# One load queue, ten transposes on TensorE, spread norms and a searched TensorE order, in a mixer-plus-MLP kernel

## The chip, the cores and the metric

The kernel runs on one core of one Trainium2 chip. The metric is the device time of one execution in microseconds. The profile shows the span from the first to the last instruction, 2.1 us (before) less than that time. Every run carries a state, fast or slow, set against the fastest run of the same kernel in the same group of runs. The engines are TensorE (PE), VectorE (DVE), ScalarE (ACT), GpSimd (POOL) and SyncE (SP); SyncE only issues DMAs here.

## The reference, cut to what matters

```python
B, S, D, F = 1, 2048, 512, 1792           # bf16 throughout
h  = gelu(layernorm(x) @ w1)              # [2048, 512]
hs = shifted(h) @ w2                      # each quarter of h moved by 1, -1, 2, -2 tokens
x1 = x + hs
out = x1 + gelu(layernorm(x1) @ w3) @ w4  # w3 [512, 1792], w4 [1792, 512]
```

The 2048 tokens are 16 tiles of 128. In units of one 128x128 by 128x512 matmul the four products need 64 + 64 + 224 + 224 = 576.

## The kernel before

Each tile is normalized (statistics on VectorE, the reciprocal root on ScalarE for tiles 0 to 3 and on GpSimd for the rest), transposed so that the features lie on partitions, multiplied ("up"), passed through GELU on ScalarE, and multiplied again ("mix" in layer 1, "down" in layer 2). A small list scheduler fixes the order of every engine. PE's order is given by a script; the other engines are ordered by a priority and a rough model of durations. Engines run their lists strictly in order.

```python
PE_TP = (0, 1, 2, 3, 4, 5)      # these tiles are transposed by PE, all others by DMA
NORM_ACT = (6, 7)               # these norms run on ScalarE, all others on VectorE
SCRIPT = """
warm:9 tp:0 warm:3 tp:1 up1:0 up1:1 tp:2-3 up1:2 mix:0-1 tp:4-5 up1:3 mix:2-3 up1:4 up2:0 mix:4-5 up2:1 mix:6
up1:5 down:0 mix:7 down:1-3 up2:2 mix:8 up1:6 ...      # cut
"""
...
loads = [load_x("sp", 0, 1), load_x("sp", 1, 1), load_w("sp", "w1", w1_sb, w1, 0, 2),
         load_w("sp", "w1", w1_sb, w1, 2, 4), load_x("sp", 2, 1), load_x("sp", 3, 1),
         load_x("sp", 4, 2), load_x("sp", 6, 2), load_w("sp", "w2", w2_sb, w2, 0, DC)]
...
load_w("pool", "w3", w3_sb, w3, 0, DC, after=[(("x", 1), 0)])
load_x("pool", 8, 4, after=[(("x", 7), 0)])
load_x("pool", 12, 4, after=[(("w3", 0), 0)])
load_w("pool", "w4", w4_sb, w4, 0, 7, after=[(("xT", 2, 1), 0)])
load_w("pool", "w4", w4_sb, w4, 7, 14, after=[(("xT", 2, 1), 0)])
```

`up1:g` and `up2:g` are the up-projections of a group of tiles in layers 1 and 2. `up2:0` covers tiles 0 and 1, `up2:1` tiles 2 and 3. "warm" are useless matmuls that keep PE busy until data come. DMA transposes are issued by SyncE, in the same queue as its loads.

## Time and profile before

| | before |
|---|---|
| time, median of the first 4 runs | 153.74 us (150.10 to 157.47) |
| span of the profiled run, its mean clock | 151.6 us, 0.966 |
| PE busy | 137.7 us, 91% |
| 576 matmuls at 216 ns | 124.3 us |
| start of the second w3 group (`up2:1`) | 39.06 us |

First the busy line and the slices of the page of the kernel before. The slices cut the span into 40 equal parts of 3.79 us; a digit is the busy share in tenths, and PEclk is the granted clock.

```profile
PE 137.7 (91%) x730; PEld 71.0 (47%) x730; DVE 62.1 (41%) x162; ACT 45.9 (30%) x54; POOL 20.8 (14%) x43
PE   6925959996699999999999999999969999999993
DVE  2816679898913253110045866691001100012321
PEclk9997589999879999999999999999999999999999
```

PE is full from the twelfth slice to the end but for the thirtieth slice, a wait for GELU, and the last. Most of the loss lies in the first eleven slices, and in two places the clock is below 9.

Next, lines of the timeline of PE before: start, duration, engine, line, operation, output<-inputs, count, and in brackets the idle time before it and what ended it.

```profile
6.66 1.95 PE L314 MATMUL y_ps<-xnT,w_sb 128*128 128x128 bf16 x32
12.41 1.13 PE L290 MATMUL o_ps<-ident,xn_buf 128*128 128x128 bf16 x8 [3.80 <-DVE xn_buf L275]
14.23 3.60 PE L314 MATMUL y_ps<-xnT,w_sb 128*128 128x256 bf16 x16 [0.69 <-ACT xnT L295]
22.83 1.92 PE L314 MATMUL y_ps<-xnT,w_sb 128*128 128x256 bf16 x16 [1.05 <-ACT xnT L295]
39.06 1.14 PE L314 MATMUL y_ps<-x1nT,w_sb 128*128 128x256 bf16 x9 [2.57 <-DMA x1nT<-xn_buf]
112.67 6.20 PE L378 MATMUL o_ps<-w_sb,h2T 128*128 128x512 bf16 x28 [1.21 <-ACT h2T L329]
```

The 3.80 us gap waits for the norm of tile 2. The same 16 matmuls take 3.60 us at 14.23 and 1.92 us at 22.83: the first time the clock is at half. The 2.57 us gap before `up2:1` waits for a DMA transpose. (The line at 39.06 is cut off by the end of the view's window at 40 us: the whole group is 56 matmuls and takes 7.94 us in the chain of waits.)

Why the norm of tile 2 came so late is read from VectorE's timeline of the kernel before:

```profile
5.90 0.69 DVE L247 BATCH_NORM_STATS2 st<-x_sb 128x6 f32<-128x512 bf16 x1
6.86 0.69 DVE L247 BATCH_NORM_STATS2 st<-x_sb 128x6 f32<-128x512 bf16 x1
11.15 0.69 DVE L247 BATCH_NORM_STATS2 st<-x_sb 128x6 f32<-128x512 bf16 x1 [3.38 <-DMA x_sb<-in_x_dram]
11.95 0.41 DVE L275 TENSOR_SCALAR xn_buf<-x_sb,mv,rstd 128x512 bf16<-128x512 bf16 x1
```

The statistics of tiles 2 and 3 were done by 7.6 us, and ScalarE had their roots by 8.1 us.

Two lines of the chain that ended last, before (start, duration, what), name the causes of the two gaps:

```profile
3.64 7.49 DMA x_sb<-in_x_dram
31.87 7.06 DMA x1nT<-xn_buf
```

The first is the 256 KB piece of x, which shared the DMA engines with w3. The second is one transposed tile, landing while w4 was loading.

### The profile page before, as it was taken

What the parts mean: (1) busy time and instruction counts of PE and PEld (TensorE: products, weight loads), DVE (VectorE), ACT (ScalarE), POOL (GpSimd) and SP (SyncE); (2) the same over time, 40 slices, a digit from 0 to 9 for tenths busy, and PEclk for the clock granted to TensorE, in tenths of its full rate; (3) what the DMA queues carried; (4) which work ended last, traced back from release to release, by engine and by line L of the source; (5) the groups of instructions that cost most, each with busy time, mean ns of one, the idle gap of its engine ahead of it and who ended that gap; (6) DMA issues with size and microseconds to landing.
All of it is one profiled execution on the core that took longest, in us unless ns stands there. A gap on an engine that the chain in (4) does not pass through costs nothing.

```text
span 151.6 us, 1850 instructions
## 1 busy us (share of the span) xinstructions
PE 137.7 (91%) x730; PEld 71.0 (47%) x730; DVE 62.1 (41%) x162; ACT 45.9 (30%) x54; POOL 20.8 (14%) x43
## 2 busy tenths in 40 slices
PE   6925959996699999999999999999969999999993
PEld 2523525882576444444444444444424444444462
DVE  2816679898913253110045866691001100012321
ACT  3545272253043500036644000025540165500000
POOL 2100633651510101000000121111000000000000
PEclk9997589999879999999999999999999999999999
DMA  3997455399942312110001123223000200011111
GB/s 111 295 361 267 142 174 89 55 276 255 164 97 43 61 42 47 60 36 0 0 0 35 33 71 74 69 69 69 0 0 5 69 0 0 0 35 35 35 49 54
DMA packets 19830, 12.42 MB, mean 82 GB/s; under 512 B 14640, under 2 KB 18864, under 8 KB 19824
## 3 DMA queue, kind: packets, MB, share of 16 engines
q1 hardware_dynamic: 18784, 7.61, 21.1%
q0 software_dynamic: 1040, 4.72, 10.1%
q8 instruction: 5, 0.08, 0.2%
q14 instruction: 1, 0.01, 0.0%
HBM read 6.82 MB, written 2.10 MB: 59 GB/s over the span
## 4 chain that ended last, share of the span: by engine, by line
PE 76%; DMA 11%; DVE 5%; SPq 2%; POOL 1%; issue 1%; ACT 1%
PE y_ps L314 36%; PE o_ps L378 32%; PE o_ps L354 8%; DMA x1nT<-xn_buf 6%; DMA x_sb<-in_x_dram 5%; DVE st L247 2%; DVE xn_buf L275 2%; SPq L234 1%; POOL rstd L262 1%; ACT h2T L329 1%; POOL w_sb L239 1%; SPq L239 1%; DVE x_sb L360 0%; PE o_ps L290 0%; ACT xnT L295 0%
## 5 line engine op out<-in xcount | busy, mean ns | idle before, releaser
L314 PE MATMUL y_ps<-x1nT,w_sb 128*128 128x512 bf16 (+1 forms) x280 | 51.0, 345 | 2.6 <-DMA x1nT<-xn_buf 2.6
L378 PE MATMUL o_ps<-w_sb,h2T 128*128 128x512 bf16 (+1 forms) x238 | 49.7, 367 | 1.2 <-ACT h2T L329 1.2
L329 ACT ACTIVATE h2T<-y_ps 128x1024 bf16<-128x1024 f32 (+1 forms) x29 | 28.6, 994 | 64.7 <-PE y_ps L314 64.7
L314 PEld LDWEIGHTS y_ps<-x1nT,w_sb 128*128 128x128 bf16 x280 | 28.2, 101 | 24.9 <-issue 3.0
L378 PEld LDWEIGHTS o_ps<-w_sb,h2T 128*128 128x128 bf16 x238 | 22.8, 98 | 27.6 <-issue 1.7
L386 DVE TENSOR_TENSOR o_sb<-o_ps,x_sb 128x512 bf16<-128x512 f32 (+1 forms) x17 | 11.2, 660 | 52.2 <-PE o_ps L378 52.2
L262 POOL TENSOR_TENSOR rstd<-vpe,neghalf 128x1 f32<-128x1 f32 x28 | 15.7, 563 | 66.8 <-DVE vpe L259 66.6
L247 DVE BATCH_NORM_STATS2 st<-x_sb 128x6 f32<-128x512 bf16 x32 | 22.0, 686 | 5.4 <-DMA x_sb<-in_x_dram 5.2
L360 DVE TENSOR_TENSOR x_sb<-o_ps,x_sb 128x512 bf16<-128x512 f32 x16 | 11.1, 691 | 21.8 <-PE o_ps L354 21.6
L314 PE MATMUL y_ps<-xnT,w_sb 128*128 128x256 bf16 (+2 forms) x112 | 16.6, 309 | 1.7 <-ACT xnT L295 1.7
L354 PE MATMUL o_ps<-w_sb,hT 128*128 128x512 bf16 x64 | 17.0, 399 | 0.3 <-ACT hT L329 0.3
L275 DVE TENSOR_SCALAR xn_buf<-x_sb,mv,rstd 128x512 bf16<-128x512 bf16 x30 | 12.1, 405 | 5.5 <-POOL rstd L262 5.4
L314 PEld LDWEIGHTS y_ps<-xnT,w_sb 128*128 128x128 bf16 x112 | 10.3, 105 | 7.4 <-ACT xnT L295 2.2
L329 ACT ACTIVATE hT<-y_ps 128x1024 bf16<-128x1024 f32 (+1 forms) x9 | 8.3, 930 | 12.5 <-PE y_ps L314 12.5
L354 PEld LDWEIGHTS o_ps<-w_sb,hT 128*128 128x128 bf16 x64 | 6.4, 103 | 8.3 <-issue 1.1
L290 PE MATMUL o_ps<-ident,xn_buf 128*128 128x128 bf16 x24 | 2.8, 250 | 4.5 <-DVE xn_buf L275 3.8
L402 PE MATMUL o_ps<-zeros 128*128 128x512 bf16 x12 | 5.2, 601 | 1.2 <-DVE zeros L220 1.2
L249 DVE BATCH_NORM_AGGREGATE mv<-st 128x2 f32<-128x6 f32 x32 | 5.8, 180 | 0.9
L295 ACT ACTIVATE xnT<-o_ps 128x512 bf16<-128x512 bf16 x6 | 3.6, 593 | 5.2 <-PE o_ps L290 5.0
L290 PEld LDWEIGHTS o_ps<-ident,xn_buf 128*128 128x128 bf16 x24 | 1.8, 110 | 6.2 <-DVE xn_buf L275 5.1
L259 DVE TENSOR_SCALAR vpe<-mv 128x1 f32<-128x1 f32 x28 | 4.1, 151 | 0.6
L239 POOL DMA_DIRECT2D w_sb<-in_w_dram x3 | 2.8, 949 | 4.2 <-DMA x1nT<-xn_buf 2.2
(21 smaller groups left out, 11.5 us busy)
## 6 DMA issues: line engine op xcount, KB each, us to landing
out_dram<-o_sb SPq DMA_DIRECT2D x15, 128.0 KB, 1.7
w_sb<-in_w_dram POOLq DMA_DIRECT2D x1, 1792.0 KB, 11.1
w_sb<-in_w_dram POOLq DMA_DIRECT2D x2, 896.0 KB, 6.9
x_sb<-in_x_dram POOLq DMA_DIRECT2D x2, 512.0 KB, 4.6
x_sb<-in_x_dram SPq DMA_DIRECT2D x4, 128.0 KB, 2.7
w_sb<-in_w_dram SPq DMA_DIRECT2D x2, 256.0 KB, 3.3
x_sb<-in_x_dram SPq DMA_DIRECT2D x2, 256.0 KB, 9.1
w_sb<-in_w_dram SPq DMA_DIRECT2D x1, 512.0 KB, 11.4
```

The source lines that it names most:

```text
L239: lambda e: e.dma_start(dst[:, c0:c1, :], src.rearrange("(c p) f -> p c f", p=P)[:, c0:c1, :]),
L247: pg.add("dve", f"bnst{q}", lambda e: e.bn_stats(st6[:, q, :], src), reads=[(rs, 0)], writes=[(("st6", q), 0)], dur=620)
L249: pg.add("dve", f"bnag{q}", lambda e: e.bn_aggr(mv[:, q, :], st6[:, q, :]), reads=[(("st6", q), 0)], writes=[(("mv", q), 0)], dur=130)
L262: lambda e: e.tensor_tensor(rstd[:, q : q + 1], vpe[:, q : q + 1], neghalf[:], ALU.pow),
L275: lambda e: e.tensor_scalar(xn_buf[:, q % NXN, :], src, mv[:, q, 0:1], rstd[:, q : q + 1], ALU.subtract, ALU.mult),
L314: ins = e.matmul(y_ps[:, p, W * i : W * (i + 1)], wsb[:, dc, P * fc : P * (fc + 1)], src[:, dc, P * t0 : P * t0 + W], start=(dc == 0), sto ...
L329: (lambda d, s: (lambda e: e.activation(d, s, ACT_F.Gelu_apprx_tanh)))(dst, ysrc),
L354: ins = e.matmul(dst, hT[:, j, c0 : c0 + P], w2_sb[:, j, :], start=(j == 0), stop=(j == DC - 1))
L360: lambda e: e.tensor_tensor(x1_sb[:, t, :], dst, x_sb[:, t, :], ALU.add),
L378: ins = e.matmul(dst, h2T[:, fc, P * t : P * (t + 1)], w4_sb[:, fc, cs], start=(fc == 0), stop=(fc == FC - 1))
L386: (lambda d, c: (lambda e: e.tensor_tensor(o_sb[:, oi, c], d, x1_sb[:, t, c], ALU.add)))(dst, cs),
L402: ins = e.matmul(o_ps[:, b, :], zeros[:, 0:P], zeros[:], start=True, stop=True)
```

## The change

Its intent: put all loads into one queue in order of first use; keep the transposes that the head needs off that queue by giving them to PE; spread the norms of the head over VectorE, GpSimd and ScalarE; and replace the PE order by one found by an offline search, with priorities of the other engines reckoned back from when PE needs each result. (The change speaks of the first twelve transposes; the code gives ten to PE: tiles 0 to 7 of layer 1, and tiles 0 and 1 of layer 2, which it numbers 16 and 17.) Besides these four parts the change moves the roots of tiles 2 and 3 from ScalarE to GpSimd (`NHEAD` from 4 to 2) and refits the durations of the scheduler's model.

The diff, cut to the lines that matter:

```diff
+    DUE = 6000.0     # priority of an op = when PE needs it, counted back through the graph (cut)
-    NHEAD = 4
+    NHEAD = 2
+GROUPS = {1: (1, 1, 1, 1, 2, 2, 4, 4), 2: (2, 2, 4, 4, 4)}
+NORM = {0: "pool", 4: "act", 5: "pool", 6: "pool", 7: "act", 8: "pool", 9: "pool", 10: "act", 11: "act", 16: "pool", 19: "pool", 20: "act", 21: "act"}
+EVAC = {3: "dve", 5: "dve", 7: "dve", 16: "dve", 17: "dve"}
 SCRIPT = """
-warm:9 tp:0 warm:3 tp:1 up1:0 up1:1 tp:2-3 up1:2 mix:0-1 tp:4-5 up1:3 mix:2-3 up1:4 up2:0 mix:4-5 up2:1 mix:6
-up1:5 down:0 mix:7 down:1-3 up2:2 mix:8 up1:6 mix:9-10 down:4 ...
+warm:3 warm:9 ty:1 ty:0 up1:1 tp:2 up1:0 tp:3 up1:2 mix:0 ty:5 up1:3 mix:1 ty:4 mix:2 ty:7 ty:6 up1:4-5
+ty:16-17 mix:3-4 up2:0 mix:5 up2:1 down:0 mix:6 up1:6 down:3 mix:7 mix:9-10 up1:7 mix:8 down:1 ...
 """
-        loads = [load_x("sp", 0, 1), load_x("sp", 1, 1), load_w("sp", "w1", w1_sb, w1, 0, 2), ...
-        load_w("pool", "w3", ...); load_x("pool", 8, 4, ...); load_x("pool", 12, 4, ...); load_w("pool", "w4", ...) x2
+        loads = [load_x("sp", t, 1) for t in range(4)]
+        loads += [load_w("sp", "w1", w1_sb, w1, 0, 2), load_w("sp", "w1", w1_sb, w1, 2, 4), load_x("sp", 4, 2),
+                  load_x("sp", 6, 2), load_w("sp", "w2", w2_sb, w2, 0, DC), load_w("sp", "w3", w3_sb, w3, 0, DC),
+                  load_x("sp", 8, 4), load_x("sp", 12, 4), load_w("sp", "w4", w4_sb, w4, 0, 7),
+                  load_w("sp", "w4", w4_sb, w4, 7, 14)]
```

`ty` is a PE transpose that writes into a buffer of the up-projections (`y_ps`); `tp` writes into one of the two banks that mix and down use (`o_ps`).

More of the change, by code (lines that the diff above doesn't have):

```diff
@@ L26 @@
 class Program:
-    SYNC = 180.0
+    HOP = {"pe": 190.0, "dve": 160.0, "act": 230.0, "pool": 200.0, "sp": 70.0}
     LOOK = {"dve": 300.0, "act": 300.0}
+    DUE = 6000.0
     def __init__(self):
@@ L102, in order @@
         assert seen == len(self.ops), "cycle"
+        if self.DUE:
+            topo, left = [], [len(d) for d in preds]
+            stack = [i for i, n in enumerate(left) if n == 0]
+            while stack:
+                i = stack.pop()
+                topo.append(i)
+                for j in succs[i]:
+                    left[j] -= 1
+                    if left[j] == 0:
+                        stack.append(j)
+            due, t = {}, self.DUE
+            for op in self.ops:
+                if op.eng == "pe" and not op.name.startswith("warm"):
+                    due[op.idx] = t
+                    t += op.dur
+            for i in reversed(topo):
+                op = self.ops[i]
+                late = due.get(i, 1e9)
+                for j in succs[i]:
+                    o = self.ops[j]
+                    hop = 70.0 if op.queue else (self.HOP[op.eng] if o.eng != op.eng else 120.0)
+                    work = (2300.0 if op.queue == "tp" else op.dur + 1850.0) if op.queue else op.dur
+                    late = min(late, o.prio - hop - work)
+                op.prio = late
         for op in self.ops:
@@ L105, in order @@
                 op.prio = op.first
+        self.preds = preds
         npend = [len(d) for d in preds]
@@ L112, in order @@
                 cands[op.eng].append(op)
-        free = {e: 0.0 for e in ENGINES}
+        free = {e: 560.0 for e in ENGINES}
         qfree = 0.0
@@ L129, in order @@
             if op.queue is None:
-                free[e] = start + op.dur
-                done = free[e]
-            else:
-                issue = 1300.0 if op.queue == "tp" else (1100.0 if e == "pool" else 460.0)
-                free[e] = start + issue
+                done = free[e] = start + op.dur
+            else:
+                free[e] = start + (1300.0 if op.queue == "tp" else (1000.0 if e == "pool" else 460.0))
                 if op.queue == "tp":
-                    done = start + 2400.0
+                    done = max(start + 2300.0, qfree + 1200.0)
                 else:
-                    qfree = max(qfree, start + 700.0) + op.dur
-                    done = qfree + 1500.0
+                    qfree = max(qfree, start + 1500.0) + op.dur
+                    done = qfree + 350.0
             out.append(op)
@@ L143, in order @@
                 o = self.ops[j]
-                ready[j] = max(ready[j], done + (60.0 if (o.eng == e and op.queue is None) else self.SYNC))
+                hop = 70.0 if op.queue else (self.HOP[e] if o.eng != e else (0.0 if e == "pe" else 120.0))
+                ready[j] = max(ready[j], done + hop)
                 if npend[j] == 0:
@@ L149, in order @@
         return out
+GROUPS = {1: (1, 1, 1, 1, 2, 2, 4, 4), 2: (2, 2, 4, 4, 4)}
+NORM = {0: "pool", 4: "act", 5: "pool", 6: "pool", 7: "act", 8: "pool", 9: "pool", 10: "act", 11: "act", 16: "pool", 19: "pool", 20: "act", 21: "act"}
+EVAC = {3: "dve", 5: "dve", 7: "dve", 16: "dve", 17: "dve"}
 SCRIPT = """
-warm:9 tp:0 warm:3 tp:1 up1:0 up1:1 tp:2-3 up1:2 mix:0-1 tp:4-5 up1:3 mix:2-3 up1:4 up2:0 mix:4-5 up2:1 mix:6
-up1:5 down:0 mix:7 down:1-3 up2:2 mix:8 up1:6 mix:9-10 down:4 mix:11 down:5 mix:12 down:6 mix:13 down:7 mix:14-15
-up2:3 down:8-9 up2:4 down:10-15
+warm:3 warm:9 ty:1 ty:0 up1:1 tp:2 up1:0 tp:3 up1:2 mix:0 ty:5 up1:3 mix:1 ty:4 mix:2 ty:7 ty:6 up1:4-5
+ty:16-17 mix:3-4 up2:0 mix:5 up2:1 down:0 mix:6 up1:6 down:3 mix:7 mix:9-10 up1:7 mix:8 down:1 mix:14 up2:2
+mix:15 mix:13 mix:11 down:7 down:2 down:6 down:5 mix:12 up2:3 down:4 down:11 down:10 up2:4 down:8 down:14
+down:12 down:9 down:13 down:15
 """
@@ L161, in bass_standalone__mixer_s_mlp__prompt_kernel @@
     NT, DC, FC = S // P, D // P, F // P
-    GROUPS = {1: [(0, 1), (1, 1), (2, 2), (4, 2), (6, 2)] + [(t, 4) for t in range(8, NT, 4)],
-              2: [(0, 2), (2, 2)] + [(t, 4) for t in range(4, NT, 4)]}
-    NHEAD = 4
-    PE_TP = (0, 1, 2, 3, 4, 5)
+    groups = {l: [(sum(GROUPS[l][:i]), n) for i, n in enumerate(GROUPS[l])] for l in GROUPS}
+    NHEAD = 2
     NXN, NO, NPAIR, NOB = 12, 4, 3, 2
     SHIFT = (1, -1, 2, -2)
-    NORM_ACT = (6, 7)
     HTW = S + 4
-    group_of = {(l, t): g for l in (1, 2) for g, (t0, n) in enumerate(GROUPS[l]) for t in range(t0, t0 + n)}
+    group_of = {(l, t): g for l in (1, 2) for g, (t0, n) in enumerate(groups[l]) for t in range(t0, t0 + n)}
     xt = x[0].rearrange("(t p) d -> p t d", p=P)
@@ L202, in bass_standalone__mixer_s_mlp__prompt_kernel @@
         o_bf = o_ps[:, :, :].bitcast(BF16)
+        y_bf = y_ps[:, :, :].bitcast(BF16)
         pg = Program()
@@ L240, in load_w @@
                    reads=list(after), writes=[((name, c), 0) for c in range(c0, c1)],
-                   dur=(c1 - c0) * P * src.shape[1] * 2 / 320.0, queue=eng)
+                   dur=(c1 - c0) * P * src.shape[1] * 2 / 330.0, queue=eng)
         def ln(layer, t):
@@ L247, in ln @@
             pg.add("dve", f"bnst{q}", lambda e: e.bn_stats(st6[:, q, :], src),
-                   reads=[(rs, 0)], writes=[(("st6", q), 0)], dur=620)
+                   reads=[(rs, 0)], writes=[(("st6", q), 0)], dur=605)
             pg.add("dve", f"bnag{q}", lambda e: e.bn_aggr(mv[:, q, :], st6[:, q, :]),
-                   reads=[(("st6", q), 0)], writes=[(("mv", q), 0)], dur=130)
+                   reads=[(("st6", q), 0)], writes=[(("mv", q), 0)], dur=75)
             if q < NHEAD:
@@ L253, in ln @@
                        lambda e: e.activation(sdv[:, q : q + 1], mv[:, q, 1:2], ACT_F.Sqrt, bias=eps_c[:], scale=1.0),
-                       reads=[(("mv", q), 0), (("eps",), 0), (("warm",), 0)], writes=[(("sdv", q), 0)], dur=280)
+                       reads=[(("mv", q), 0), (("eps",), 0), (("warm",), 0)], writes=[(("sdv", q), 0)], dur=190)
                 pg.add("dve", f"rcp{q}", lambda e: e.reciprocal(rstd[:, q : q + 1], sdv[:, q : q + 1]),
-                       reads=[(("sdv", q), 0)], writes=[(("rstd", q), 0)], dur=100)
+                       reads=[(("sdv", q), 0)], writes=[(("rstd", q), 0)], dur=75)
             else:
@@ L259, in ln @@
                        lambda e: e.tensor_scalar(vpe[:, q : q + 1], mv[:, q, 1:2], LN_EPS, None, ALU.add),
-                       reads=[(("mv", q), 0)], writes=[(("vpe", q), 0)], dur=100)
+                       reads=[(("mv", q), 0)], writes=[(("vpe", q), 0)], dur=70)
                 pg.add("pool", f"rstd{q}",
                        lambda e: e.tensor_tensor(rstd[:, q : q + 1], vpe[:, q : q + 1], neghalf[:], ALU.pow),
-                       reads=[(("vpe", q), 0), (("neghalf",), 0)], writes=[(("rstd", q), 0)], dur=720)
-            if q in NORM_ACT:
+                       reads=[(("vpe", q), 0), (("neghalf",), 0)], writes=[(("rstd", q), 0)], dur=470)
+            how = NORM.get(q, "dve")
+            dst = xn_buf[:, q % NXN, :]
+            if how == "dve":
+                pg.add("dve", f"norm{q}",
+                       lambda e: e.tensor_scalar(dst, src, mv[:, q, 0:1], rstd[:, q : q + 1], ALU.subtract, ALU.mult),
+                       reads=[(rs, 0), (("mv", q), 0), (("rstd", q), 0)], writes=[(("xn", q % NXN), q)], dur=330)
+            else:
                 pg.add("dve", f"nmr{q}",
@@ L267, in ln @@
                                                  ALU.mult, ALU.mult),
-                       reads=[(("mv", q), 0), (("rstd", q), 0)], writes=[(("nmr", q), 0)], dur=100)
-                pg.add("act", f"norm{q}",
-                       lambda e: e.activation(xn_buf[:, q % NXN, :], src, ACT_F.Identity,
-                                              bias=nmr[:, q : q + 1], scale=rstd[:, q : q + 1]),
-                       reads=[(rs, 0), (("nmr", q), 0), (("rstd", q), 0)], writes=[(("xn", q % NXN), q)], dur=740)
-            else:
-                pg.add("dve", f"norm{q}",
-                       lambda e: e.tensor_scalar(xn_buf[:, q % NXN, :], src, mv[:, q, 0:1], rstd[:, q : q + 1],
-                                                 ALU.subtract, ALU.mult),
-                       reads=[(rs, 0), (("mv", q), 0), (("rstd", q), 0)], writes=[(("xn", q % NXN), q)], dur=360)
@@ L278, in ln @@
-            if layer == 2 or t not in PE_TP:
-                dst = xnT if layer == 1 else x1nT
-                pg.add("sp", f"tp{q}",
-                       lambda e: e.dma_start(dst[:, :, P * t : P * (t + 1)], xn_buf[:, q % NXN, :], transpose=True),
-                       reads=[(("xn", q % NXN), q)], writes=[(("xT", layer, t), 0)], queue="tp")
-        def pe_transpose(t):
-            b, v = next_bank()
-            dst = o_bf[:, b, 0:D]
+                       reads=[(("mv", q), 0), (("rstd", q), 0)], writes=[(("nmr", q), 0)], dur=130)
@@ new lines, in ln @@
+                if how == "act":
+                    f = lambda e: e.activation(dst, src, ACT_F.Identity, bias=nmr[:, q : q + 1],
+                                               scale=rstd[:, q : q + 1])
+                else:
+                    f = lambda e: e.tensor_scalar(dst, src, rstd[:, q : q + 1], nmr[:, q : q + 1], ALU.mult, ALU.add)
+                pg.add(how, f"norm{q}", f, reads=[(rs, 0), (("nmr", q), 0), (("rstd", q), 0)],
+                       writes=[(("xn", q % NXN), q)], dur=710 if how == "act" else 760)
@@ new lines, in ln, with pe_transpose @@
+            if q not in pe_tp:
+                xT = xnT if layer == 1 else x1nT
+                pg.add("sp", f"tp{q}",
+                       lambda e: e.dma_start(xT[:, :, P * t : P * (t + 1)], xn_buf[:, q % NXN, :], transpose=True),
+                       reads=[(("xn", q % NXN), q)], writes=[(("xT", layer, t), 0)], queue="tp")
+        def pe_transpose(t, q, pair):
+            layer = 1 if q < NT else 2
+            if pair:
+                b, v = next_pair()
+                dst, res = y_bf[:, b, 0:D], ("y", b)
+            else:
+                b, v = next_bank()
+                dst, res = o_bf[:, b, 0:D], ("o", b)
@@ L288, in f @@
             def f(e):
                 for c in range(DC):
-                    ins = e.transpose(dst[:, P * c : P * (c + 1)], xn_buf[:, t, P * c : P * (c + 1)], ident[:])
+                    ins = e.transpose(dst[:, P * c : P * (c + 1)], xn_buf[:, q % NXN, P * c : P * (c + 1)], ident[:])
                 return ins
-            pg.add("pe", f"htp{t}", f, reads=[(("xn", t), t), (("ident",), 1)], writes=[(("o", b), v)], dur=450)
-            pg.add("act", f"hev{t}",
-                   lambda e: e.activation(xnT[:, :, P * t : P * (t + 1)],
-                                          dst.rearrange("p (c s) -> p c s", c=DC), ACT_F.Copy),
-                   reads=[(("o", b), v)], writes=[(("xT", 1, t), 0)], dur=560)
+            pg.add("pe", f"tp{q}", f, reads=[(("xn", q % NXN), q), (("ident",), 1)], writes=[(res, v)], dur=225)
@@ new lines, in pe_transpose @@
+            to = (xnT if layer == 1 else x1nT)[:, :, P * t : P * (t + 1)]
+            frm = dst.rearrange("p (c s) -> p c s", c=DC)
+            if EVAC.get(q, "act") == "act":
+                pg.add("act", f"ev{q}", lambda e: e.activation(to, frm, ACT_F.Copy),
+                       reads=[(res, v)], writes=[(("xT", layer, t), 0)], dur=480)
+            else:
+                pg.add("dve", f"ev{q}", lambda e: e.tensor_copy(to, frm),
+                       reads=[(res, v)], writes=[(("xT", layer, t), 0)], dur=335)
@@ L300, in mm_up @@
         def mm_up(layer, g):
-            t0, n = GROUPS[layer][g]
+            t0, n = groups[layer][g]
             W = n * P
@@ L319, in mm_up @@
                        reads=[((wn, c), 0) for c in range(DC)] + [(("xT", layer, t), 0) for t in range(t0, t0 + n)],
-                       writes=[(("y", p), v)], dur=k * DC * W * 0.4222)
+                       writes=[(("y", p), v)], dur=k * DC * (W * 0.4167 + 2.5))
                 ysrc = y_ps[:, p, 0 : k * W].rearrange("p (i s) -> p i s", i=k)
@@ L329, in mm_up @@
                        (lambda d, s: (lambda e: e.activation(d, s, ACT_F.Gelu_apprx_tanh)))(dst, ysrc),
-                       reads=[(("y", p), v), (("warm",), 1)], writes=wr, dur=60 + k * W * 0.833)
+                       reads=[(("y", p), v), (("warm",), 1)], writes=wr, dur=50 + k * W * 0.833)
                 yield
@@ L357, in mm_mix @@
             pg.add("pe", f"mix{t}", f, reads=[(("w2", c), 0) for c in range(DC)] + sorted(need, key=str),
-                   writes=[(("o", b), v)], dur=DC * 216)
+                   writes=[(("o", b), v)], dur=DC * 215.5)
             pg.add("dve", f"x1_{t}",
                    lambda e: e.tensor_tensor(x1_sb[:, t, :], dst, x_sb[:, t, :], ALU.add),
-                   reads=[(("o", b), v), (("x", t), 0)], writes=[(("x1", t), 0)], dur=640)
+                   reads=[(("o", b), v), (("x", t), 0)], writes=[(("x1", t), 0)], dur=600)
             ln(2, t)
@@ L383, in mm_down @@
                        reads=[(("w4", c), 0) for c in range(FC)] + [(("h2", j, g), 0) for j in range(FC)],
-                       writes=[(("o", b), v)], dur=FC * W * 0.4222)
+                       writes=[(("o", b), v)], dur=FC * (W * 0.4167 + 2.5))
                 pg.add("dve", f"res{t}_{hh}",
                        (lambda d, c: (lambda e: e.tensor_tensor(o_sb[:, oi, c], d, x1_sb[:, t, c], ALU.add)))(dst, cs),
-                       reads=[(("o", b), v), (("x1", t), 0)], writes=[(("osb", oi, hh), t)], dur=100 + W * 1.05)
+                       reads=[(("o", b), v), (("x1", t), 0)], writes=[(("osb", oi, hh), t)], dur=70 + W * 1.04)
                 pg.add("sp", f"out_dma{t}_{hh}",
@@ L405, in warm_pe @@
             nwarm[0] += 1
-            pg.add("pe", f"warm{nwarm[0]}", f, reads=[(("zeros",), 0)], writes=[(("o", b), v)], dur=n * 300)
+            pg.add("pe", f"warm{nwarm[0]}", f, reads=[(("zeros",), 0)], writes=[(("o", b), v)], dur=n * 427)
             next_bank()
@@ L412, in bass_standalone__mixer_s_mlp__prompt_kernel @@
                reads=[(("eps",), 0)] + [(("sdv", q), 0) for q in range(NHEAD)], writes=[(("warm",), 1)], dur=1400)
-        loads = [load_x("sp", 0, 1), load_x("sp", 1, 1), load_w("sp", "w1", w1_sb, w1, 0, 2),
-                 load_w("sp", "w1", w1_sb, w1, 2, 4), load_x("sp", 2, 1), load_x("sp", 3, 1),
-                 load_x("sp", 4, 2), load_x("sp", 6, 2), load_w("sp", "w2", w2_sb, w2, 0, DC)]
+        loads = [load_x("sp", t, 1) for t in range(4)]
[3 more added lines that the diff above has]
+                  load_w("sp", "w4", w4_sb, w4, 7, 14)]
@@ L416, in bass_standalone__mixer_s_mlp__prompt_kernel @@
         for i, op in enumerate(loads):
             op.first = i - 100
-        load_w("pool", "w3", w3_sb, w3, 0, DC, after=[(("x", 1), 0)])
-        load_x("pool", 8, 4, after=[(("x", 7), 0)])
-        load_x("pool", 12, 4, after=[(("w3", 0), 0)])
-        load_w("pool", "w4", w4_sb, w4, 0, 7, after=[(("xT", 2, 1), 0)])
-        load_w("pool", "w4", w4_sb, w4, 7, 14, after=[(("xT", 2, 1), 0)])
+        steps = []
+        for step in SCRIPT.split():
+            kind, n = step.split(":")
+            a, _, b = n.partition("-")
+            steps += [(kind, n) for n in (range(int(a), int(b or a) + 1) if kind != "warm" else [int(n)])]
@@ L423, in bass_standalone__mixer_s_mlp__prompt_kernel @@
+        pe_tp = {n for kind, n in steps if kind in ("tp", "ty")}
         for t in range(NT):
             ln(1, t)
-        script = SCRIPT
-        for step in script.split():
-            kind, n = step.split(":")
+        for kind, n in steps:
             if kind == "warm":
-                warm_pe(int(n))
-                continue
-            a, _, b = n.partition("-")
-            for n in range(int(a), int(b or a) + 1):
-                if kind == "tp":
-                    pe_transpose(n)
-                elif kind == "mix":
-                    mm_mix(n)
-                elif kind == "down":
-                    mm_down(n)
-                else:
-                    for _ in mm_up(int(kind[2]), n):
-                        pass
+                warm_pe(n)
+            elif kind in ("tp", "ty"):
+                pe_transpose(n % NT, n, kind == "ty")
+            elif kind == "mix":
+                mm_mix(n)
+            elif kind == "down":
+                mm_down(n)
+            else:
+                for _ in mm_up(int(kind[2]), n):
+                    pass
```

## The prediction

> **What bounds it now.** TensorE. The page gives PE 137.7 us busy of a 151.6 us span. The work equals 576 matmuls of 128x512; the timeline shows 56 of them in 12.09 us, 216 ns each, the spacing that the Trainium skill gives for the full clock ("TensorE: Matmul & The Clock Gate", section on the 2.5 ns floor); this trace agrees. So dense work is 576 x 216 ns = 124.3 us, plus 2 us of transposes. The rest is head, gaps and clock:
> - The chain of waits has x_sb arriving 7.5 us after its issue; tile 2's statistics start at 11.15 us, and the timeline shows PE idle 8.6 to 12.4 us.
> - The same page says an idle PE falls to half clock. This trace has half clock from 13.0 to 19.8 us, after that gap (16 matmuls of 256 columns took 3.6 us there, 1.92 later; 2.9 us lost in all), and from 40.3 to 43.7 us, after a 2.57 us wait for a DMA transpose (1.7 us lost). That transpose ran against w4's load: 7.06 us of the chain.
> - By 39.06 us PE had done only 84 of the 576 equivalents (18 us dense). The other 492 took 110.1 us against 106.2 dense.
>
> **What the change does.** All loads go in one queue in order of use: x0-x3 and w1 (1 MB) no longer compete with w3. The first DMA records show about 250 KB/us for 1 KB rows; from 2 us on that puts x0-x3 at 4.1, w1 at 6.3, x4-x7 at 8.3, w2 at 10.4, w3 near 16, x8-x15 near 20, w4 at 26-27 us. DMA transposes queue behind them, so the first ten (not twelve: 40 small matmuls in the instruction order) tiles go to PE: 16 more transposes of 56 ns, 1 us. VectorE loses 13 norms (405 ns each, 5.3 us), gains 5 evacuations[...]; GpSimd [...]and ScalarE (0.81 us) take the norms.
>
> **The new head with those durations (an estimate).** Warm matmuls end at 6.3 us; first up-projection 7.4; second 8.8; third 9.8; first mix 11.3; the single tiles end near 16, tiles 4-7 near 20; the first w3 group runs 22-28; its second group starts at 29 to 30.5 us instead of 39.06. From there 106.2 us dense, 1 us of small losses as before, 0.5-1 us of bank waits, and 2.5 us from the last matmul to the end as before: span about 140. Run time is 2 us above the span, as before (153.7 and 151.6): **142.0 us**, range 138 to 147. So 9-10 us come from the head, 1.7 from the second half-clock stretch, 1.2 from a GELU wait at 111.5 us that the new order hides.
>
> Chances: faster by over 2% 0.94, within 2% 0.05, slower 0.01.
>
> **What would show it.** PE's slices at 6 or more from 7 us on, 9 from 20 us on, no gap over 2 us; no half-clock stretch after 6 us; second w3 group starting at 28-31 us; w4 landed by 28 us; PE share near 96% of a span near 140.
>
> **What would make it wrong.** The short pieces of the head could bring another half-clock stretch (1.7 to 3.4 us). GpSimd norms could be slower than 1 us and delay the reciprocal roots behind them (1-3 us). One queue may move less than 250 KB/us, so that w4 and the transposes behind it come after 30 us. The times before scatter (150.1 to 157.5), and so will the ratio.

## The result, and the profile after

The changed kernel took 139.81 us in the median of four runs (139.46 to 140.05). The ratio of the fast runs is 0.928, with a 95% interval of 0.921 to 0.935: faster. Ratios are the mean time of one kernel's fast runs over the mean of the other's fast runs of the same rounds, so they are not quite the ratio of the medians quoted.

The page after. It has no PEclk row, since this trace holds no clock records; in e10, the same kernel run again, the records show the full clock from 6.31 us to the end:

```profile
PE 132.0 (96%) x762; PEld 70.1 (51%) x762; DVE 60.1 (44%) x167; ACT 47.5 (35%) x56; POOL 22.4 (16%) x47
PE   6689999999999999999999999999999999999992
DVE  2979899997170798710097327100222000122231
```

PE now fills from the fourth slice on. The timeline of PE after, at the places that answer to those above:

```profile
7.08 1.05 PE L355 MATMUL y_ps<-xnT,w_sb 128*128 128x128 bf16 x16
8.65 0.40 PE L327 MATMUL o_ps<-ident,xn_buf 128*128 128x128 bf16 x4 [0.52 <-DVE xn_buf L296]
11.31 1.04 PE L395 MATMUL o_ps<-w_sb,hT 128*128 128x512 bf16 x4 [0.26 <-DMA w_sb<-in_w_dram]
28.35 6.28 PE L355 MATMUL y_ps<-x1nT,w_sb 128*128 128x256 bf16 x56
```

The last gap is the short one before 11.31 us, a wait for w2; from there on the timeline shows no gap. The chain after says the same: it runs through loads until 11.3 us and then through PE to the end.

```profile
4.60 6.67 DMA w_sb<-in_w_dram
28.51 6.11 PE y_ps L355 x56
116.84 18.18 PE o_ps L419 x98
```

The profile of the kernel before is of a run of 153.69 us. It lies 2.5 to 3.6 us above the two fast runs on which the ratio rests (150.10 and 151.19 us). So the two profiles differ by 14.1 us of span, the fast runs by 10.9 us of time; what follows splits the 14.1 us.

Where the 14.1 us of span came from: the second w3 group starts at 28.51 instead of 39.06 us, with the same 84 matmul equivalents done before it. That is 10.5 us. From there to the end it was 112.5 us before (151.6 - 39.06) and is 109.0 us now (137.5 - 28.51): 3.5 us. Of these, 1.7 us are half of the 3.41 us at half clock after the 2.57 us gap, and 1.2 us are the wait for GELU at 111.5 us; the other 0.6 us are not accounted for.

The clock before and after, by stretch of the span (stretch, length, PE busy and count, granted clock, DMA share, GB/s), first before, then after:

```profile
12.00:20.00 8.00, 6.77 (x31) 0.57 0.47 161
28.40:39.10 10.70, 8.13 (x68) 1.00 0.98 231
39.10:50.00 10.90, 10.90 (x71) 0.84 0.47 76
```

```profile
12.00:20.00 8.00, 8.00 (x84) 1.00 1.07 372
28.40:39.10 10.70, 10.70 (x79) 1.00 0.43 87
39.10:50.00 10.90, 10.90 (x52) 1.00 0.31 73
```

Before, the busy share of the DMA engines was 0.98 from 28.4 to 39.1 us, when w4 and the transposes met. After, the heavy load lies between 12 and 20 us, where PE does not wait for it.

### The profile page after: what moved, and what is told of

Read it like the earlier page. It is cut to its first block, busy times and chain, and to the rows that moved or that the text cites. A ratio compares the mean times of both kernels' runs of the same rounds, so it can differ in the third digit from the quotient of the medians.

```text
span 137.5 us, 1926 instructions
## 1 busy us (share of the span) xinstructions
PE 132.0 (96%) x762; PEld 70.1 (51%) x762; DVE 60.1 (44%) x167; ACT 47.5 (35%) x56; POOL 22.4 (16%) x47
## 4 chain that ended last, share of the span: by engine, by line
PE 90%; DMA 5%; SPq 3%; issue 0%; DVE 0%
PE y_ps L355 43%; PE o_ps L419 35%; PE o_ps L395 10%; DMA w_sb<-in_w_dram 5%; SPq L262 2%; PE y_ps L327 1%; SPq L267 1%; DVE o_sb L427 0%
## 5 line engine op out<-in xcount | busy, mean ns | idle before, releaser
L355 PE MATMUL y_ps<-x1nT,w_sb 128*128 128x512 bf16 (+1 forms) x280 | 49.3, 336 | 0.0
L401 DVE TENSOR_TENSOR x_sb<-o_ps,x_sb 128x512 bf16<-128x512 f32 x16 | 11.0, 689 | 12.4 <-PE o_ps L395 12.3
L395 PE MATMUL o_ps<-w_sb,hT 128*128 128x512 bf16 x64 | 15.8, 380 | 0.3 <-DMA w_sb<-in_w_dram 0.3
L355 PE MATMUL y_ps<-xnT,w_sb 128*128 128x128 bf16 (+2 forms) x128 | 15.1, 272 | 0.0
L296 DVE TENSOR_SCALAR xn_buf<-x_sb,mv,rstd 128x512 bf16<-128x512 bf16 x19 | 7.6, 409 | 3.2 <-POOL rstd L290 2.6
L307 POOL TENSOR_SCALAR xn_buf<-x_sb,rstd,nmr 128x512 bf16<-128x512 bf16 x7 | 5.4, 772 | 5.9 <-DVE mv L277 5.1
L443 PE MATMUL o_ps<-zeros 128*128 128x512 bf16 x12 | 4.1, 509 | 1.2 <-DVE zeros L248 1.2
L277 DVE BATCH_NORM_AGGREGATE mv<-st 128x2 f32<-128x6 f32 x32 | 4.7, 170 | 0.3
L304 ACT ACTIVATE xn_buf<-x_sb,nmr,rstd 128x512 bf16<-128x512 bf16 x6 | 4.6, 810 | 0.3 <-DVE nmr L300 0.3
L327 PE MATMUL y_ps<-ident,xn_buf 128*128 128x128 bf16 x32 | 2.8, 220 | 1.1 <-POOL xn_buf L307 0.7
L327 PEld LDWEIGHTS y_ps<-ident,xn_buf 128*128 128x128 bf16 x32 | 2.1, 98 | 2.5 <-DVE xn_buf L296 0.9
(26 smaller groups left out, 15.6 us busy)
```

Source lines behind the costliest of these rows:

```text
L277: pg.add("dve", f"bnag{q}", lambda e: e.bn_aggr(mv[:, q, :], st6[:, q, :]), reads=[(("st6", q), 0)], writes=[(("mv", q), 0)], dur=75)
L296: lambda e: e.tensor_scalar(dst, src, mv[:, q, 0:1], rstd[:, q : q + 1], ALU.subtract, ALU.mult),
L307: f = lambda e: e.tensor_scalar(dst, src, rstd[:, q : q + 1], nmr[:, q : q + 1], ALU.mult, ALU.add)
L327: ins = e.transpose(dst[:, P * c : P * (c + 1)], xn_buf[:, q % NXN, P * c : P * (c + 1)], ident[:])
L355: ins = e.matmul(y_ps[:, p, W * i : W * (i + 1)], wsb[:, dc, P * fc : P * (fc + 1)], src[:, dc, P * t0 : P * t0 + W], start=(dc == 0), sto ...
L395: ins = e.matmul(dst, hT[:, j, c0 : c0 + P], w2_sb[:, j, :], start=(j == 0), stop=(j == DC - 1))
```

## The experiments

The prediction gives one number for four changes made together. My theory was that loads and PE transposes carry the gain and need each other, that the norms relieve VectorE in the head, and that the order trims. The rivals were that one part carries it alone, above all the loads, or that the order does. Twelve runs were made, one of them of the changed kernel unaltered; all gave correct results.

| run | what | median us | median before, same rounds | ratio of fast runs | second w3 group starts |
|---|---|---|---|---|---|
| e1 | before + new loads | 149.73 | 153.97 | 0.976 | 36.66 |
| e2 | before + filled gaps, order disturbed | 157.26 | 153.97 | none given | 44.82 |
| e3 | after with the old loads | 149.05 | 153.97 | 0.968 | 37.11 |
| e4 | after, all norms on VectorE, all evacuations on ScalarE | 138.88 | 153.97 | 0.904 | 27.71 |
| e5 | before + filled gaps, order kept | 152.43 | 154.17 | 0.990 | 39.24 |
| e6 | after with the old PE order | 147.40 | 154.17 | 0.958 | 34.12 |
| e7 | after with six PE transposes | 148.75 | 154.17 | 0.965 | 39.15 |
| e10 | after, unaltered | 139.57 | 154.91 | 0.919 | 28.28 |
| e11 | e4 once more | 139.27 | 154.91 | 0.917 | 28.01 |
| e8 | e11, roots of tiles 0 and 1 on GpSimd | 139.31 | 154.91 | 0.918 | 28.16 |
| e9 | e8, w1 from ScalarE's queue | 139.99 | 154.91 | 0.922 | 28.45 |
| e12 | after without the new priorities | 140.84 | 154.10 | 0.930 | 29.40 |

The starts are read from the profiled run of each. The four groups of runs were on different chips, and the fast runs of the kernel before differ between them (150.1 and 151.2 us beside the changed kernel first, 153.5 to 154.1 beside e1), so differences under 1% are read only within a group. The ratios of e1 to e7 should not be set beside those of e8 to e12 or the 0.928 of the change: on chips 8 and 6 nearly all runs of the kernel before that are fast have a clock of 0.966, while on chips 0 and 1 its runs at that clock are slow. The medians of the changed kernel in its two groups differ less (139.81 and 139.57 us). The record labels every ratio of an experiment "unclear" and does not say why; of the intervals given, all but those of e1 (0.970 to 0.982) and e5 lie below 0.98.

### e1: the loads alone

```diff
 # in the kernel before
-        loads = [load_x("sp", 0, 1), load_x("sp", 1, 1), load_w("sp", "w1", ...
+        loads = [load_x("sp", t, 1) for t in range(4)]   # ... the list of the changed kernel
```

> The kernel before with the new load list alone (one SyncE queue, order of first use). Theory A (the parts need each other): tile 2's statistics start by 5 us instead of 11.15 and PE's first gap closes, but the DMA transposes of tiles 6, 7, 16, 17 now stand behind w4 in the same queue, so PE gets a new gap of 5 us or more that ends near 24 us; second w3 group starts near 34-35 us, time 145-149, i.e. only a third to a half of the gain. Theory B (the loads are the gain): second w3 group at 29-31 us and time 140-142.

Theory A held in kind; the second group came 2 us later than it said and the time is just over its range. The first gap (8.6 to 12.4 us) is gone, but a new one stands later. PE's timeline of e1:

```profile
19.25 1.04 PE L354 MATMUL o_ps<-w_sb,hT 128*128 128x512 bf16 x4 [0.25 <-ACT hT L329]
25.03 3.57 PE L314 MATMUL y_ps<-xnT,w_sb 128*128 128x256 bf16 x16 [4.73 <-DMA xnT<-xn_buf]
36.66 6.28 PE L314 MATMUL y_ps<-x1nT,w_sb 128*128 128x256 bf16 x56
```

The transposes of tiles 6 and 7 were issued from 14.73 us on and landed at 25 us, after the loads. The 16 matmuls after the gap ran at half clock (3.57 us again). The loads alone gave 2.4%, where e4, which is the changed kernel but for the spread of norms, gave 9.6% in the same rounds.

### e3: everything but the loads

```diff
 # in the changed kernel
-        loads = [load_x("sp", t, 1) for t in range(4)]   # ... all loads on SyncE
+        loads = [load_x("sp", 0, 1), ...                 # the lists of the kernel before, w3, x8-x15, w4 on GpSimd
```

> The changed kernel with the load list of the kernel before (w3, x8-x15 and w4 from the GpSimd queue, x2 and x3 after w1). Theory A (the load order carries the head): x2 lands near 11 us, PE has a gap of 3 us or more before it and a half-clock stretch after it, GpSimd's reciprocal roots wait behind its DMA issues; time 146-150. Rival (the PE order and the transposes on PE carry it): at most 2 us lost, below 142.

The time that theory A gave held. PE's timeline of e3 shows three gaps, a late norm, a late w2, and a DMA transpose that meets w4:

```profile
12.15 0.61 PE L327 MATMUL o_ps<-ident,xn_buf 128*128 128x128 bf16 x4 [2.49 <-DVE xn_buf L296]
16.53 1.49 PE L395 MATMUL o_ps<-w_sb,hT 128*128 128x512 bf16 x3 [2.06 <-DMA w_sb<-in_w_dram]
37.11 6.27 PE L355 MATMUL y_ps<-x1nT,w_sb 128*128 128x256 bf16 x56 [2.51 <-DMA x1nT<-xn_buf]
```

The first is the gap of the kernel before again, and here too it is not x2 that was late, as the expectation says, but x4: VectorE had the statistics of tile 2 at 6.11 us, and the norm of tile 3 stood behind those of tile 4:

```profile
11.09 0.69 DVE L275 BATCH_NORM_STATS2 st<-x_sb 128x6 f32<-128x512 bf16 x1 [2.49 <-DMA x_sb<-in_x_dram]
```

The changed kernel has the same trap, the statistics of tile 4 before the norms of tiles 2 and 3, but with the new loads x4 is there at 7.58 us. Whether a swap in VectorE's list alone would close this gap of the kernel before was not run.

### e7: six transposes on PE instead of ten

```diff
-mix:2 ty:7 ty:6 up1:4-5
-ty:16-17 mix:3-4 up2:0
+mix:2 up1:4-5
+mix:3-4 up2:0
```

> The changed kernel with only tiles 0 to 5 transposed on PE, as before; tiles 6, 7 and the first two of the second layer go back to DMA transposes. Theory A (a transpose in the one queue stands behind w4, which lands at about 23 us): PE gap of 6 us or more that ends at 24-26 us, a half-clock stretch after it, time 147-151. Rival (a transpose issued at 16 us lands in 2.5 us, whatever was queued before): below 142.

Theory A held. PE's timeline of e7 (this profile fell in a slow run; the three fast runs took 147.76 to 149.25 us):

```profile
16.76 1.91 PE L355 MATMUL y_ps<-xnT,w_sb 128*128 128x256 bf16 x16 [0.24 <-DVE vpe L287]
25.91 3.57 PE L355 MATMUL y_ps<-xnT,w_sb 128*128 128x256 bf16 x16 [7.24 <-DMA xnT<-xn_buf]
```

SyncE issued the transposes at 16.55 us. The view of this tile's DMAs gives their time to landing:

```profile
DMA to landing us min/median/max: 2.5/2.5/8.7
```

Most of these transposes land in 2.5 us; the longest, behind the loads, took 8.7 us. The Trainium skill ("DMA: Bandwidth & Descriptors", on HWDGE ordering) says each DMA engine consumes descriptors in ring order; these times agree. Four tiles moved to PE, 0.22 us each in the chain, are what lets the loads stand in one queue. (SyncE itself was still issuing w4 until 16.50 us here, and until 14.69 us in e1, so it could not have issued a transpose much earlier; how much of the loss that adds was not separated.)

### e6: the old order of PE

```diff
-GROUPS = {1: (1, 1, 1, 1, 2, 2, 4, 4), ...
+GROUPS = {1: (1, 1, 2, 2, 2, 4, 4), ...
 # SCRIPT of the kernel before, with the added transposes where they fit:
+warm:9 tp:0 warm:3 tp:1 up1:0 up1:1 tp:2-3 up1:2 mix:0-1 tp:4-5 up1:3 mix:2-3 tp:6-7 up1:4 tp:16-17 up2:0 mix:4-5 up2:1 mix:6
```

> The changed kernel with the PE order and the tile groups of the kernel before; loads in one queue, ten tiles transposed on PE and the spread of norms stay. Theory A (loads and PE transposes carry the gain, the order only trims the head): 140.5 to 143, with some PE gaps below 1.5 us before 20 us and perhaps one before a w3 group. Rival (the searched order carries it): 145 or more.

My theory fell here, and the rival held: 147.4 us, so 7.6 us more than the 139.8 of the changed kernel, though the loads and the transposes are the new ones. PE's timeline of e6:

```profile
10.95 1.92 PE L354 MATMUL y_ps<-xnT,w_sb 128*128 128x256 bf16 x16 [1.27 <-DVE xnT L336]
15.84 0.40 PE L326 MATMUL o_ps<-ident,xn_buf 128*128 128x128 bf16 x4 [0.59 <-DVE x_sb L400]
17.04 1.92 PE L354 MATMUL y_ps<-xnT,w_sb 128*128 128x256 bf16 x16 [0.81 <-DVE xnT L336]
22.11 0.40 PE L326 MATMUL o_ps<-ident,xn_buf 128*128 128x128 bf16 x4 [0.77 <-DVE x_sb L400]
106.06 6.20 PE L418 MATMUL o_ps<-w_sb,h2T 128*128 128x512 bf16 x27 [1.21 <-ACT h2T L369]
```

No gap is over 1.3 us and the clock stays at 1.0, but they add up: between 5 us and the second w3 group the timeline lists 6.2 us of gaps, against 1.9 us in the changed kernel. The old order does transpose, evacuate, up, GELU and mix of one pair of tiles in a row, so PE has nothing else to do while another engine evacuates; and its transposes use the same two banks as mix, so they wait for VectorE to add the last mix (the x_sb waits). The new order puts work of other tiles between, in one-tile groups, and writes most transposes into the buffers of the up-projections. The second w3 group starts 5.8 us later than after, and from there to the end e6 needs 110.9 us (145.0 - 34.12) where the changed kernel needs 109.1 (137.5 - 28.35; the timeline gives 28.35 where the chain gives 28.51, since pipelined matmuls overlap). In that second part the GELU wait of 1.2 us is back. e6 takes back three things at once, the order, the one-tile groups and the buffers of the transposes; which of them matters most was not run.

### e2 and e5: is the half clock a cost of its own?

```diff
 # e2, in the kernel before
-... up1:0 up1:1 tp:2-3 up1:2 ... mix:4-5 up2:1 mix:6
+... up1:0 up1:1 warm:16 tp:2-3 up1:2 ... mix:4-5 warm:11 up2:1 mix:6
 # e5 in addition
-           ... writes=[(("o", b), v)], dur=n * 300)
+           ... writes=[(("o", b), v)], dur=0.0 if n in (11, 16) else n * 300)
```

> The kernel before with useless matmuls put into its two PE gaps: 16 before the transposes of tiles 2 and 3, 11 before the second w3 group. No load, transpose or norm comes earlier. Theory A (half clock follows from the gaps, 2.9 and 1.7 us lost): no half-clock stretch after 6.5 us, time near 146-148 in every run, and the scatter of 150 to 157 is gone. Rival: the clock falls for another reason or its loss is hidden behind the arrivals: time stays 150 to 157, or is longer.

e2 failed as an experiment, and the reason is worth knowing: the scheduler reckoned 300 ns for each filling matmul, so it moved other engines' work as well. ScalarE got the norm of a later tile ahead of the GELU that PE needed, and that norm hung on GpSimd, whose list stood still behind a DMA issue that waited for x7. GpSimd and then PE in e2:

```profile
15.00 0.76 POOL L234 DMA_DIRECT2D x_sb<-in_x_dram  x1 [10.49 <-DMA x_sb<-in_x_dram]
22.05 1.89 PE L354 MATMUL o_ps<-w_sb,hT 128*128 128x512 bf16 x4 [4.52 <-ACT hT L329]
```

(Three of its four runs are slow and the profile is of one; the edit added this gap, but no time is taken from it.)

> The fill of the two PE gaps again, now without any effect on the order of the other engines: the filling matmuls cost nothing in the kernel's own scheduling model, and the instruction order differs on PE alone, by 16 and 11 useless matmuls. Theory A (the half clock follows from PE gaps and costs 2.9 and 1.7 us): no half-clock stretch after 6.5 us, data arrive as before, time 2 to 4.6 us shorter than the kernel before of the same rounds in every run. Rival (the clock's loss is hidden behind arrivals, so the clock is a symptom): under 1 us shorter.

e5 changed PE's list only. It came between the two theories: ratio 0.990, interval 0.982 to 0.997, and neither full claim held. PE's timeline of e5:

```profile
13.37 0.92 PE L290 MATMUL o_ps<-ident,xn_buf 128*128 128x128 bf16 x8 [1.62 <-DVE xn_buf L275]
14.97 3.02 PE L314 MATMUL y_ps<-xnT,w_sb 128*128 128x256 bf16 x16 [0.69 <-ACT xnT L295]
39.24 6.27 PE L314 MATMUL y_ps<-x1nT,w_sb 128*128 128x256 bf16 x56 [0.57 <-DMA x1nT<-xn_buf]
```

The first fill did not cover its gap to the end (1.62 us stayed), and the stretch at half clock shrank from 6.83 to 3.41 us (15.6 to 19.0 us). Yet the second w3 group starts at 39.24 us against 39.06. That does not show that the first stretch costs nothing, for in this run the x of tile 4 also came 0.95 us later than in the kernel before; why is not known. VectorE's timeline of e5 shows it, and the chain of e5 shows the last transpose:

```profile
12.10 0.69 DVE L247 BATCH_NORM_STATS2 st<-x_sb 128x6 f32<-128x512 bf16 x1 [4.51 <-DMA x_sb<-in_x_dram]
31.55 7.55 DMA x1nT<-xn_buf
```

From the statistics of tile 4 to the start of that transpose e5 took 19.45 us (31.55 - 12.10), the kernel before 20.72 us (31.87 - 11.15). So the chain did become 1.27 us shorter, against the 1.7 us reckoned for half of the first stretch; the later x took back 0.95 us, and the transpose, 7.55 us instead of 7.06, the rest. What the first stretch costs stays open.

The second fill left only 0.57 us of wait, no half clock followed, and the span is 1.5 us shorter (150.1 against 151.6), near the 1.7 us reckoned for that stretch; the fast runs of the same rounds differ by 1.6 us on the mean. So wherever half clock appears after the start in these traces, it comes after a PE gap, and the second stretch cost about what was reckoned. Not every gap brings it: in e3 none followed the gap of 2.51 us before 37.11 us.

### e4 and e11: are the spread norms worth anything?

```diff
-NORM = {0: "pool", 4: "act", ...}
-EVAC = {3: "dve", ...}
+NORM = {}
+EVAC = {}
```

> The changed kernel with all norms on VectorE and all evacuations of transposes on ScalarE. Theory A (VectorE is the limit between 8 and 20 us, where it is busy for 9 tenths): PE gets gaps there, time 1 to 3 us longer (141-143). Rival: the spread is off the critical path, since PE's only wait that matters is for w2 at 11.3 us: within 0.5 us of 139.8.

> The changed kernel unaltered, as the yardstick for the other three runs of this call on the same chip: 139.3 to 140.2, no half-clock stretch, PE without gaps from about 11.3 us on.

> The changed kernel with all norms on VectorE and all evacuations on ScalarE, a second time, now beside the changed kernel. Theory A (it was a real 0.7 to 0.9 us: a norm on GpSimd holds up the next reciprocal root behind it in the same engine): 0.5 to 1.0 us shorter than e10, transposes of tile 2 near 8.0 us against 8.65. Rival (it was another chip or an earlier w2): within 0.3 us of e10.

e4 was not slower, so the theory that VectorE is the limit in the head fell; it even looked 0.9 us faster. Side by side on one chip with five rounds little was left of that: e10 139.57 us (139.09 to 140.04), e11 139.27 us (138.95 to 139.50), 0.2% apart, at the edge of what the rival allowed. The mechanism that I named for e11 is in the traces. PE's lines for the transpose of tile 2, first in e10, then in e11:

```profile
9.02 0.40 PE L327 MATMUL o_ps<-ident,xn_buf 128*128 128x128 bf16 x4 [0.51 <-DVE xn_buf L296]
```

```profile
8.36 0.39 PE L327 MATMUL o_ps<-ident,xn_buf 128*128 128x128 bf16 x4
```

With the first norm on GpSimd (0.77 us there, 0.41 us on VectorE), the reciprocal root of tile 2 waits behind it, and PE gets tile 2 0.66 us later. But in the profiled runs only 0.27 us of that remained at the second w3 group. The spread of norms brings nothing; that it costs 0.3 us is likely but not shown.

### e8 and e9: a version that beats both?

```diff
 # e8, on e11
-    NHEAD = 2           # tiles 0 and 1: root on ScalarE
+    NHEAD = 0           # all roots on GpSimd; the table for the root is never loaded
 # e9, on e8
-load_w("sp", "w1", w1_sb, w1, 0, 2), load_w("sp", "w1", w1_sb, w1, 2, 4)
+load_w("act", "w1", w1_sb, w1, 0, 2), load_w("act", "w1", w1_sb, w1, 2, 4)
```

> As e11, and tiles 0 and 1 take their reciprocal root from GpSimd like all others, so ScalarE loads one function table at the start and none at 5 us; it can then evacuate the first transposes as soon as they are there. Theory A (the table load holds up the first up-projection, which waits 0.5 us for ScalarE): first up-projection at 6.5-6.7 us instead of 7.1, time 0.3-0.5 us shorter than e11. Rival (w1's landing or VectorE binds right behind it): under 0.2 us.

e8: 139.31 us, no gain over e11. In its profile the first up-projection starts at 7.00 us (7.47 in e11, 7.10 in e4), and what it won was given back to w2:

```profile
10.97 0.81 PE L395 MATMUL o_ps<-w_sb,hT 128*128 128x512 bf16 x3 [0.66 <-DMA w_sb<-in_w_dram]
```

> As e8, with the two halves of w1 issued from ScalarE's queue instead of SyncE's, so two queues feed the first 6 us. Theory A (one queue is held back by its issue rate before 4 us, 218 KB/us against 345 later): w1 and w2 land 0.5 us earlier or more and the time is 0.2-0.6 us shorter than e8. Rival (w1 takes bandwidth from x0 and x1, and PE waits for x): no gain or a loss of up to 0.5 us.

e9: 139.99 us, 0.7 us slower than e8. The wait for w2 is gone, but the first transposes come later (6.56 us against 5.83 in e8), since w1 now shares the DMA engines with x: between 3 and 5 us w1's queue moved 0.28 MB and x's queue 0.37 MB, and VectorE waited 0.30 and 0.20 us for the second and third piece of x, which it did not in e8. PE's first transposes in e9:

```profile
6.56 0.88 PE L327 MATMUL y_ps<-ident,xn_buf 128*128 128x128 bf16 x8 [0.58 <-DVE xn_buf L296]
```

The rival held, with a loss a little over its 0.5 us. The Trainium skill ("Trainium Kernel Development and Optimization", Key Constraints) says that all queues run on the same 16 DMA engines and a second issuing engine saves only issue time; this run agrees, and shows that it can cost. No version beat the changed kernel beyond doubt.

### e12: the priorities of the other engines

```diff
-    DUE = 6000.0
+    DUE = 0.0
```

> The changed kernel without the new priorities of the other engines (the due times reckoned back from the PE order); the PE order itself, loads, transposes and norms stay. 52 rows of VectorE's order move, ScalarE's not at all. Theory A (from 11 us on PE waits for nothing, so there is slack for VectorE's order): within 1 us of 139.8. Rival (the searched PE order only holds with these priorities): 141 or more, with new PE gaps on VectorE before 30 us.

140.84 us (140.42 to 141.64), about 1 us over the changed kernel on other chips, just past theory A's 1 us and short of the rival's 141. The profile has one new gap, before the transpose of tile 6:

```profile
16.52 0.40 PE L327 MATMUL y_ps<-ident,xn_buf 128*128 128x128 bf16 x4 [0.72 <-POOL xn_buf L307]
```

The norm on GpSimd that it waits for started at 15.70 us, against 14.20 us in e10; its root had waited 0.79 us for VectorE. So VectorE's order does reach PE, by way of GpSimd, as the rival said in kind. The full clock came late in this run (7.04 us by the clock records, 6.31 us in e10), but that is not the loss: the second mix starts at 13.33 us here and at 13.24 us in e10, and the second w3 group at 29.40 against 28.28 us. The priorities are worth about 1 us, with the chips as the open end.

## Why the prediction was right

- **Time.** Predicted 142.0, range 138 to 147; measured 139.81. The 2.2 us too many come from two terms of the span (predicted about 140, measured 137.5); a third, the 2 us from span to time, was 0.5 us too small and hid part of them. The rest after the second w3 group was set at 106.2 us plus 1.5 to 2 us of losses: PE needed 106.5 us from 28.51 to the last matmul at 135.0, so there are hardly any losses. And the second group was set at 29 to 30.5 us and came at 28.5.
- **The head.** Predicted first up-projection 7.4, second 8.8, third 9.8, first mix 11.3, second w3 group 29-30.5; measured 7.1, 8.9, 10.0, 11.3, 28.5. The load rate of 250 KB/us held only at first: the DMA view gives 239 KB/us from 2 to 4 us, 310 from 4 to 9 us and 352 from 15 to 22 us. So w4 landed near 23.5 us, not 26-27, and no transpose was waited for.
- **The causes.** The load collisions in both gaps were named rightly, and e3 and e7 show that the gaps come back when their remedies are taken out. One step of the first was wrong: "tile 2's statistics start at 11.15 us". Those were tile 4's; x2 was there before 5.9 us, and the norm of tile 2 was held up by VectorE's list order. The remedy was the same, since x4 was late for the reason given; that the misread step did no harm is partly luck: the changed kernel keeps the trap in VectorE's list, and the same loads happen to bring x4 early too (7.58 us). The half clock at 13.0 to 19.8 us was listed at 2.9 us lost; what it cost stays open (e5). The sum does not depend on it, since that loss was counted inside the head and not again.
- **What it did not say.** The prediction gives the new PE order no worth of its own but the 1.2 us of the GELU wait. e6 shows that the order, with its groups and buffers, is worth about as much as each other part. Taken out one at a time, the loads cost 9.2 us (10.2 us against e4 on the same chip), the four transposes 8.9 us and the order 7.6 us (medians less 139.81): together 25.7 us, far more than the whole gain (13.9 us by the medians, 10.9 us by the fast runs; the runs were on different chips, so each may be off by 1 us or so). They are not terms of a sum. PE starts a piece when the last of its inputs is there, so each part alone is capped by the other two; e1, the loads alone, won 2.4%. The transposes alone and the order alone were not run on the kernel before.
- **What was wrong in the reasons.** The spread of norms was given as relief for VectorE. e4 and e11 show no gain from it. The fear that norms on GpSimd delay the roots behind them was right in kind, 0.66 us at tile 2, under the 1-3 us named.
- **The scatter.** The changed kernel's runs (139.09 to 140.05 us in ten runs) lie within 1 us of each other, at a clock of 0.999 to 1.0. The kernel before scatters from 150 to 157 us with clocks of 0.989 down to 0.955. With five rounds its runs at 0.977 took 151.1 to 152.8 us and those at 0.955 to 0.956 took 155.2 to 156.9 us. The latter are slow and are left out of the ratio, so the ratio is, if anything, on the careful side. The clock comes in steps: the profiles with one stretch of 3.41 us at half clock have 0.989 (e5), with two 0.977 (e1, e3), with three 0.965 to 0.967 (before, e2, e7). An estimate from this: the slowest runs of the kernel before, at 0.956, had four, and the changed kernel, by the records of e10, none after its start.

## What to carry to other kernels

In the head of a kernel a piece starts when its last input arrives, so each part of a change can be needed and none enough: walk the order tile by tile with measured durations instead of adding up gains, and look at which instruction stands in front of a late one in its own engine's list. When loads go into one queue, move whatever must overtake them, such as a DMA transpose, off that queue first. And when an experiment inserts work into a scheduled kernel, compare the instruction order of all engines before believing it.

## What the Trainium skill lacked or had wrong

- "TensorE: Matmul & The Clock Gate" advises no PE gaps over about 3 us. Here half clock followed a gap of 2.57 us (before) and, in e5, gaps of 1.62 and 0.69 us close together; none followed a gap of 2.51 us in e3 or the gaps up to 1.27 us in e6. So the length of the gap alone did not decide. (The page also tells of frequent short idles that bring the half clock, in its section on a second failure mode, without lengths.) The lengths of the half-clock stretches before, 6.83 and 3.41 us, agree with the page's 3413 ns window.
- The same page puts the first release of the clock at about 4 us of activity, give or take 0.5 us, though it also tells of one kernel with 6, 11 or 14 matmuls at half clock. Here the clock records put it 3.2 us (e7) to 5.9 us (e2, e12) after the first matmul, a spread nearer to the second. The twelve warm matmuls of the changed kernel took 4.07 us in its profile and 5.28 us in e10, and the first transpose started at 5.63 and 6.26 us.
- "DMA: Bandwidth & Descriptors" has no figure for a transpose behind queued loads: 2.5 us for most transposes of e7, 8.7 us for the one behind w4, 7.06 us beside a w4 load from another queue before.
- "TensorE: Matmul & The Clock Gate" reckons the penalty of half clock as half its duration. For the second stretch that is 1.7 us, and e5 gained 1.5 us of span without it, so the page agrees there; for half of the first stretch it is 1.7 us as well, and the chain of e5 became 1.27 us shorter, all of which a later x and a longer transpose took back.
